# Linear attention and a gated feed-forward layer in one kernel: more of the matrix products in seven sub-products, set 5 turned by TensorE, and another order of the work

## The chip, the cores and the metric

The kernel runs on one core of one Trainium2 chip. The metric is the device time of one execution in microseconds (us); lower is better. Engines are named as in the profile: PE is TensorE's matmul, PEld its weight load, DVE is VectorE, ACT is ScalarE, POOL is GpSimd, SP is SyncE.

## The reference

Cut to what matters:

```python
# q, k, v: (4, 8, 768, 64) float32; lam: (8,); moe_w_in: (512, 2048); moe_w_out: (2048, 512)
for b in range(12):                                   # blocks of 64 tokens
    qb, kb, vb = (q[:, :, sl], k[:, :, sl], v[:, :, sl])
    intra = einsum('bhic,bhjc->bhij', qb, kb) * Dmask  # Dmask = lam ** (i - j) below the diagonal
    intra = einsum('bhij,bhjd->bhid', intra, vb)
    inter = einsum('bhid,bhde->bhie', qb * lam_pow, kv_state)
    out[:, :, sl] = intra + inter
    kv_state = lam_block * kv_state + einsum('bhsd,bhse->bhde', kb * rev_pow, vb)
x = out.transpose(0, 2, 1, 3).reshape(3072, 512)
h = x @ w_in                                          # 512 -> 2048
g = h * (1.0 / (1.0 + exp(-h)))                       # silu
y = g @ w_out                                         # 2048 -> 512, float32, the output
```

## The kernel before

Work is in **units** of 128 tokens, (n, b): pair n of blocks of batch b, six pairs for each of four batches, 24 units. Attention is done in 12 **sets** of two units: sets 0 to 3 hold the units (0, b) and (1, b) of batch b, whose state is carried within the set; sets 4 to 11 hold two batches of one n. The feed-forward layer's first product is done in **groups**: four groups of two units (256 columns), then four of four units (512 columns), one for each n from 2 to 5; what the text calls block 4 is the group with n = 4, and the last block the one with n = 5.

Stages of a set. The loads of q, k and v (`raw`, L380) are issued on SP's queue. `kq` holds k and scaled q in bf16 (casts and multiplications on DVE or ACT), `vd` the scaled v (L349, two halves). `kqT` is kq turned: sets before TURNED = 5 by TensorE transposes (`tr`, L513 for the paired sets, L693 for later ones) and copies from PSUM by DVE and ACT; the others by a DMA transpose on SP's queue (L702). `d_ps` is the state's increment (L534), `y` and `xf` the running states in float32, `xe` the states cast to bf16 (on ACT, DVE or POOL), `st_ps` the scores, which DVE multiplies by the mask into `st` (L349). `x_ps` is the attention's output (L614 and L619 for paired sets, L759 and L767 for the others; L619 and L767 hold the part from the states), copied to `xt`.

First product, L905: `h_ps` over 4 steps of 128 rows of w_in; silu on ACT (L917) makes `g`. The last group (n = 5) is done **in seven**: both operands are split into quadrants, and seven products of quadrants or of sums of quadrants, 128 matmul rows by 256 columns each (L1023), give the four quadrants of the result after some additions. The sums S1 to S4 of w_in's quadrants are tiles `wsum`, the sums T1 to T4 of xt's are `xsum`; part-results are kept as `m` and added to `h`.

Second product: units 0 to 7 (PLAIN = 8) plainly, 16 matmuls of 512 columns a unit (`o_ps`, L940). The other 16 units in seven, four units at a time (L1153): sums of g (`s`, and S3 in place in `g`) by DVE, sums of w_out (`wsum`, halves of 128 x 1024). Results go out through `osb` by DMAs on ACT's queue.

Every step is entered into a planner as a task with a key, its possible engines with their costs, its buffers and what it depends on. The planner simulates the engines and three DMA queues and at each step takes the ready task with the least key whose buffers are free; the result is one list, written out as each engine's order. Engines run in that order at run time. Costs such as those of DMA kinds (SMALL, LARGE, ...), the opening constants (SLOW, FIRST) and the keys therefore set the order, not the time itself. Where PE has nothing ready in the opening, filler matmuls of the identity (L1236) are put in.

The weights are loaded by POOL's queue (L409), each load held behind a small POOL instruction that reads a tile whose landing it awaits (L360); SP's queue is held in the same way by a small DMA. The order of the loads is one string:

```python
SEQUENCE = "s0 i0@0.2 s1 i1a@0.2 i1b i2 i3 o0 o1 s2@1.2 o2 o3 s3 s4"
```

(s is a set's loads, i and o are parts of w_in and w_out.)

Of the kernel before, what the change touches and what calls it, by code (L numbers as in the profile page):

```python
# [216 lines left out]
def kernel(  # L217
# [27 lines left out]
    FRESH, TURNED, ALONE, LEAD = 4, 5, 6, 6.5  # L245
# [3 lines left out]
    BY_POOL, IN_BY_POOL, PLAIN, SPARED = (), (), 8, 1  # L249
# [4 lines left out]
    SCORED, SOON, VD_ON, HALVED = (0, 1), 3, {"DVE": 0.7}, 0  # L254
    EAGER, CALM, ON = 8.0, 1.0, 6.0
# [94 lines left out]


# [16 lines left out]
    def load_set(key, si):  # L368
        n, b = sets[si][0]
        nb = 2  # L370
        rs = [Buf("rb") if si >= CASTING and i == 0 else None if si >= CASTING and i == 1 else Buf("ra" if si in (0, 3) else "rb")
              for i in range(3)]
        ts = []
        x = [t[b, :, 0:2 * U, :].rearrange("h (p e) d -> p h (e d)", e=2) if n < PAIRED else
             t[b:b + 2, :, n * U:n * U + U, :].rearrange("b h s d -> s (b h) d") for t in (k, q, v)]

        def go(e, i):
            if n < PAIRED:
                tile_of(rs[i], [128, H, 2, 64], F32, "raw")
                nc.sync.dma_start(out=rs[i].tile.rearrange("p h e d -> p h (e d)"), in_=x[i])  # L380
            elif si >= CASTING and i < 2:
                tl = tile_of(rs[0], [128, 2, 2, NP, 2, 64], BF16, "kq")
                nc.gpsimd.dma_start(out=tl[:, i].rearrange("p b m h d -> p (b m h) d"), in_=x[i])
            else:
                nc.sync.dma_start(out=tile_of(rs[i], [128, 2 * H, 64], F32, "raw"), in_=x[i])

        for i in (1, 0, 2) if si in QUERIES else range(3):
            if si >= CASTING and i < 2:
                t = pool_task(add((key, i), {"POOL": 0.8}, lambda e, i=i: go(e, i), bufs=[rs[0]], nbytes=0.524, kind=CAST,
                                  prior=pool_last[-1:] + raw[si - 1][1][2], late=2.0))  # L390
                ts.append([t])
                continue
            ts.append([add((key, len(ts)), {"SP": 0.55}, lambda e, i=i: go(e, i), bufs=[rs[i]], nbytes=0.524, prior=sp_last[-1:],
                           kind=WIDE if n < PAIRED else SMALL, late=0.3 if si < FRESH else 3.0)])
# [7 lines left out]
    def load_w(key, what, j, part):  # L402
        def go(e):
# [3 lines left out]
            else:  # L407
# [4 lines left out]
                          HALF if part else LARGE, prior=pool_last[-1:], late=1.0))  # L412
# [7 lines left out]
    for m, x in enumerate(SEQUENCE.split() + [f"s{i}" for i in range(len(sets))]):  # L420
# [59 lines left out]
    def prepare_2(o, rs, lk, lq, lv):  # L480
# [5 lines left out]
        def cast(e, i, a):  # L486
            src = rs[i].tile[:, :, a, :].rearrange("p (m h) d -> p m h d", h=2)
            if i:
# [5 lines left out]
        o.ck = [[add((s - (2.95 if i and o.si in SCALED else 1.0), i), {"DVE": 0.7} if i else {"DVE": 0.45, "ACT": 0.63}, lambda e, i=i, a=a: cast(e, i, a),  # L494
# [3 lines left out]
        def scale_v(e, a):  # L498
            hs = slice(4 * a, 4 * a + 4)
            tt(e, o.vd_of()[:, hs].rearrange("p h e d -> p (h e) d"), rs[2].tile[:, hs].rearrange("p h e d -> p (h e) d"),  # L500
               lam_v2[:, hs].rearrange("p h e -> p (h e)")[:, :, None].to_broadcast([128, 8, 64]), AL.mult)

        o.cv = [add((s - 0.8, 0), VD_ON, lambda e, a=a: scale_v(e, a), deps=lv, bufs=[rs[2], o.vd]) for a in range(2)]
# [19 lines left out]
    def first_2(o):  # L523
# [26 lines left out]
        def blocks(xe, i, src, t, buf):  # L550
# [5 lines left out]
            return [add((s - 0.9, 5), {"POOL": 0.5, "ACT": 0.42}, lambda e, r=r: go(e, r), deps=[t], bufs=[xe, buf])  # L556
# [9 lines left out]
        def rest():  # L566
# [6 lines left out]
            t2 = add((s - 0.9, 5), {"DVE": 0.42}, lambda e: tt(e, xf_of(), y.tile, rate, AL.mult), deps=[t1], bufs=[y, xf_n])  # L573
# [5 lines left out]
        deps = [t for t in o.turned]  # L579
        o.masked = []  # L580
        for g in range(2):
# [9 lines left out]
            ts = add((s - 0.5, g), {"PE": 0.4}, scores, deps=deps, bufs=st_ps[g] + [o.kqT])  # L591
# [42 lines left out]
    def prepare(si):  # L634
# [28 lines left out]
        def cast(e, j, i):  # L663
            src = rs[i].tile[:, j * H:j * H + H, :]
            dst = kq_of()[:, i, j].rearrange("p m h d -> p (m h) d")
            if i:
# [4 lines left out]
        ck = [[add((s - 1.0, i), {"DVE": 0.7} if i else {"DVE": 0.45, "ACT": 0.63}, lambda e, j=j, i=i: cast(e, j, i),  # L671
# [4 lines left out]
        def scale_v(e, j):  # L676
            tt(e, vd_of()[:, j], rs[2].tile[:, j * H:j * H + H, :], lam_v[:, :, None].to_broadcast([128, H, 64]), AL.mult)

        cv = [add((s - 0.8, 0), VD_ON, lambda e, j=j: scale_v(e, j),
# [114 lines left out]
    def after_first(o, t):  # L794
# [20 lines left out]
        def blocks(b, src, deps, bufs, i):  # L815
# [6 lines left out]
            return [add((s - 0.9, i), {"POOL": 0.25 + w / 1000, "ACT": 0.2 + w / 1200, "DVE": 0.1 + w / 1900}, lambda e, r=r: go(e, r),  # L822
# [65 lines left out]
    def product1(gi):  # L888
# [5 lines left out]
        for m0 in range(0, KO, 2 * per):  # L894
# [69 lines left out]
    def sums_of_w_in():  # L964
        bufs = {name: Buf("kq") if i else Buf("rb") for i, name in enumerate(("S1", "S2", "S3", "S4"))}
# [4 lines left out]

        every = [t for o in infos if rank[o.n, o.bs[0]] < SUMS_AFTER for t in o.cv] + [t for o in infos[:CASTING] for ts in o.ck for t in ts]

        def total(name, a, b, op, deps, on):
            done[name] = [add((on, 8), {"POOL": 2.4} if name in IN_BY_POOL else {"DVE": 0.7}, lambda e, ks=ks: tt(
                e, W[name]()[:, ks], W[a]()[:, ks], W[b]()[:, ks], op), deps=deps, bufs=[bufs[name]])
# [9 lines left out]
    def product1_spared(gi, wbufs, wdone):  # L985
# [20 lines left out]
        total("T1", "B12", "B11", AL.subtract, done["T3"], [])  # L1006
        total("T4", "B21", "T2", AL.subtract, done["T2"], [two])
        for jp in range(4):
            P, R = Buf("bank"), Buf("bank")
            held = [P, R, Buf("sp")]  # L1010
# [24 lines left out]
            narrow = {"22": Buf("vd"), "12": Buf("st")}  # L1035
# [175 lines left out]
    for gi in range(len(groups) - SPARED):  # L1211
        product1(gi)
# [60 lines left out]
```

## Time and profile before

| | us |
|---|---|
| median of 3 runs | 204.46 |
| lowest and highest run | 204.32, 205.02 |
| the profiled execution | 204.46 |
| its span | 202.4 |
| PE busy (share of the span) | 188.1 (93%) |
| DVE busy | 135.5 (67%) |
| ACT busy | 114.2 (56%) |
| POOL busy | 21.8 (11%) |

Every profile row is one group or one piece of the kernel's timeline. Rows of the chain of waits read: start in us, length in us, engine, tile, line, and how many instructions. Rows of the groups read: line, engine, operation, tiles out<-in, shape, count, then busy us and the mean ns of one, then the idle time before them with what ended it. Rows of the timeline read: start, length, engine, line, operation, and in brackets the idle time before it. A matmul's busy time in the groups includes its drain, which overlaps the next one; what a matmul costs in a stream is read from the chain.

### The profile page before, as it was taken

How to read it: one execution, taken by the hardware profiler on the slowest of the kernel's cores; microseconds unless marked ns; L12 is line 12 of the kernel's file. 1: busy time of each engine (PE TensorE's matmuls, PEld its weight loads, DVE VectorE, ACT ScalarE, POOL GpSimd, SP SyncE). 2: the span in 40 equal slices, each digit the busy share in tenths (PEclk: the TensorE clock that was granted, in tenths of full speed). 3: DMA queues.
4: the chain of work that ended last, by engine and by line, in shares of the span. 5: the costliest groups of instructions: out<-in, count | busy, mean ns of one | idle time of the engine just before them, and what ended most of it. 6: DMA issues, size and time to landing. Idle time of an engine off the chain costs nothing.

```text
span 202.4 us, 5779 instructions
## 1 busy us (share of the span) xinstructions
PE 188.1 (93%) x2494; PEld 135.0 (67%) x2512; DVE 135.5 (67%) x269; ACT 114.2 (56%) x207; POOL 21.8 (11%) x48
## 2 busy tenths in 40 slices
PE   0588999999999999999999999999999999999992
PEld 0476788557678655544488746486676778888881
DVE  6499620595997950969999774999577553646511
ACT  3836666327567642357764394945656575685320
POOL 6093100310110100001011000110200000000000
PEclk9999999999999999999999999999999999999998
DMA  3999999999999989999999999948001111003313
GB/s 94 301 274 202 216 215 250 254 193 212 239 269 242 206 204 261 174 267 212 202 142 231 253 194 222 225 104 160 2 3 55 52 52 36 19 0 107 104 50 108
DMA packets 87067, 33.40 MB, mean 165 GB/s; under 512 B 65026, under 2 KB 86018, under 8 KB 87042
## 3 DMA queue, kind: packets, MB, share of 16 engines
q1 hardware_dynamic: 77154, 23.07, 57.0%
q0 software_dynamic: 4752, 4.19, 12.9%
q10 hardware_dynamic: 5136, 5.77, 8.9%
q8 instruction: 19, 0.31, 0.7%
q14 instruction: 6, 0.05, 0.1%
HBM read 27.27 MB, written 6.29 MB: 166 GB/s over the span
## 4 chain that ended last, share of the span: by engine, by line
PE 84%; DVE 6%; DMA 4%; ACT 3%; issue 1%; DVEq 0%; SPq 0%
PE h_ps L905 33%; PE o_ps L1153 22%; PE o_ps L940 14%; PE h_ps L1023 6%; DMA raw<-in_k_dram 3%; DVE st L349 2%; PE x_ps L767 2%; PE d_ps L727 1%; PE tr L513 1%; PE x_ps L759 1%; DVE vd L349 1%; PE st_ps L737 1%; DMA out_dram<-osb 1%; ACT xt L342 1%; DVE kqT L344 1%
## 5 line engine op out<-in xcount | busy, mean ns | idle before, releaser
L905 PE MATMUL h_ps<-xt,w_in_bf 128*128 128x256 bf16 (+1 forms) x440 | 73.7, 317 | 0.7 <-ACT xt L342 0.3
L905 PEld LDWEIGHTS <-w_in_bf 128*128 128x128 bf16 x448 | 42.9, 98 | 24.9 <-issue 0.3
L917 ACT ACTIVATE g<-h_ps 128x512 bf16<-128x512 f32 x80 | 46.8, 595 | 20.9 <-PE h_ps L905 20.3
L940 PE MATMUL o_ps<-w_out_bf,g 128*128 128x512 bf16 x118 | 28.6, 379 | 0.8 <-issue 0.5
L1153 PEld LDWEIGHTS <-g 128*128 128x128 bf16 x256 | 25.0, 98 | 3.7
L349 DVE TENSOR_TENSOR st<-st_ps,tri 128x512 bf16<-128x512 f32 x32 | 20.3, 682 | 9.3 <-PE st_ps L737 9.3
L1153 PEld LDWEIGHTS <-s 128*128 128x128 bf16 x192 | 18.7, 98 | 2.8
L349 DVE TENSOR_TENSOR kq<-raw,lam_q 128x512 bf16<-128x512 f32 x24 | 16.3, 698 | 6.2 <-DMA raw<-in_q_dram 4.5
L940 PEld LDWEIGHTS <-g 128*128 128x128 bf16 x128 | 12.0, 98 | 12.0
L349 DVE TENSOR_TENSOR osb<-o_ps,m 128x512 f32<-128x512 f32 (+1 forms) x15 | 8.6, 581 | 13.4 <-ACT m L342 8.6
L342 ACT ACTIVATE xt<-x_ps 128x512 bf16<-128x512 f32 x16 | 9.7, 631 | 12.3 <-PE x_ps L767 9.2
L349 DVE TENSOR_TENSOR vd<-raw,lam_v 128x512 bf16<-128x512 f32 x24 | 15.7, 682 | 0.7 <-DMA raw<-in_v_dram 0.7
L1153 PE MATMUL o_ps<-w_out_bf,s 128*128 128x256 bf16 x128 | 15.3, 273 | 0.0
L1153 PE MATMUL o_ps<-wsum,g 128*128 128x256 bf16 x128 | 15.1, 273 | 0.0
L1153 PE MATMUL o_ps<-w_out_bf,g 128*128 128x256 bf16 x128 | 14.8, 273 | 0.0
L342 ACT ACTIVATE osb<-o_ps 128x512 f32<-128x512 f32 (+1 forms) x13 | 7.3, 564 | 12.7 <-PE o_ps L940 8.6
L349 DVE TENSOR_TENSOR s<-g 128x512 bf16<-128x512 bf16 x16 | 7.2, 447 | 10.8 <-ACT g L917 8.1
L342 ACT ACTIVATE m<-o_ps 128x512 f32<-128x512 f32 (+1 forms) x13 | 6.7, 515 | 13.1 <-PE o_ps L1153 12.9
L513 PE MATMUL tr<-ident,kq 128*128 128x128 bf16 x64 | 6.1, 241 | 7.7 <-DVE kq L349 7.5
L342 ACT ACTIVATE kq<-raw 128x512 bf16<-128x512 f32 x14 | 8.4, 624 | 4.5 <-DMA raw<-in_k_dram 4.0
L346 POOL CAST xe<-xf 64x256 bf16<-64x256 f32 (+1 forms) x8 | 5.1, 640 | 49.4 <-DVE xf L349 39.3
L513 PEld LDWEIGHTS <-kq 128*128 128x128 bf16 x64 | 4.6, 107 | 8.4 <-DVE kq L349 7.9
(90 smaller groups left out, 225.0 us busy)
## 6 DMA issues: line engine op xcount, KB each, us to landing
raw<-in_q_dram SPq DMA_DIRECT2D x12, 512.0 KB, 8.2
raw<-in_k_dram SPq DMA_DIRECT2D x12, 512.0 KB, 7.9
raw<-in_v_dram SPq DMA_DIRECT2D x12, 512.0 KB, 7.2
out_dram<-osb ACTq DMA_DIRECT2D x20, 256.0 KB, 4.2
w_out_bf<-in_moe_w_out_dram POOLq DMA_DIRECT2D x4, 512.0 KB, 14.9
w_in_bf<-in_moe_w_in_dram POOLq DMA_DIRECT2D x3, 512.0 KB, 11.7
w_in_bf<-in_moe_w_in_dram POOLq DMA_DIRECT2D x2, 256.0 KB, 8.2
out_dram<-osb ACTq DMA_DIRECT2D x4, 128.0 KB, 1.7
```

Source lines behind the costliest of these rows:

```text
L342: nc.scalar.activation(o, i, AF.Copy)
L344: nc.vector.tensor_copy(o, i)
L346: nc.gpsimd.tensor_copy(o, i)
L349: (nc.vector if e == "DVE" else nc.gpsimd).tensor_tensor(o, a, b, op=op)
L513: nc.tensor.transpose(t[:, m, a], o.kq_of()[:, i, m, a], ident)
L727: nc.tensor.matmul(d_of(c)[rp, j, m, :], lhsT=o.kq_of()[r, 0, j, m, p, :], rhs=o.vd_of()[r, j, 2 * m + p, :], start=j == 0 and m == 0, sto ...
L767: nc.tensor.matmul(x_of(c)[:, j, m, :], lhsT=o.xe[c].tile[:, (bs[0] + j) % 2, m, :], rhs=o.kqT_of()[:, 1, j, m, halves[c]], start=False, s ...
L905: nc.tensor.matmul(t[:, j, :], lhsT=w_in_bf[:, ko, 128 * (m1 + j):128 * (m1 + j) + 128], rhs=xt[gi].tile[:, ko, :], start=(ko == 0), stop= ...
L917: nc.scalar.activation(t[:, half * per:half * per + per], bank.tile, AF.Silu)
L940: nc.tensor.matmul(t, lhsT=g.tile[:, j, 128 * gp:128 * gp + 128], rhs=w_out_bf[:, ko, :], start=(ko == 0), stop=(ko == KO - 1))
L1023: nc.tensor.matmul(t[:, j, :], lhsT=W[w]()[:, k2, f:f + 128], rhs=X(r)[:, k2, :], start=first and j == 0 and k2 == 0, stop=True, skip_grou ...
L1153: nc.tensor.matmul(t[:, i_, :], lhsT=src(j)[:, k2, 128 * r:128 * r + 128], rhs=W[w]()[:, 2 * j + k2, :], start=first and i_ == 0 and j == ...
```

## The change

* Units 4 to 7 go from the plain second product to the one in seven (PLAIN from 8 to 4).
* Half of block 4's first product (the index pairs 0 and 1, MIXED) is done in seven, the rest as before; `product1` takes the list of row tiles, `product1_spared` the list of its parts.
* TURNED goes from 5 to 6: set 5 is turned by TensorE.
* Casts of states to bf16 have no GpSimd among their engines (XE_2, XE_B, XE_P).
* The keys of later sets are moved back by two (LEAD), the sums of w_out forward (ON from 6 to 0), the second step of a state's update back (LAZY).
* Scores depend on the turned halves they read and not on all of them (FINE).
* Costs in the planner change: LARGE, PART, SLOW, FIRST, SAFE, and the small DMA that holds SP's queue.
* Buffers: kept part-results of block 4 lie in other pools than those of the last block; T1 of xt has a tile of its own where it was made in place; three of the four sums of w_in lie in rb.

The diff, cut to its core:

```diff
-SMALL, WIDE, CAST, LARGE, HALF, TURN = (256, 17.5, 20.0), (512, 25.0, 28.0), (256, 14.0, 31.0), (2048, 88.0, 90.0), (1024, 58.0, 58.0), (1024, 50.0, 50.0)
+SMALL, WIDE, CAST, LARGE, HALF, TURN, PART = (256, 17.5, 20.0), (512, 25.0, 28.0), (256, 14.0, 31.0), (2048, 86.0, 86.0), (1024, 58.0, 58.0), (1024, 50.0, 50.0), (1024, 45.0, 45.0)
...
-    SLOW, SLOWER = 15.5, 1.8
+    SLOW, SLOWER = 14.0, 1.8
...
-    FIRST, LAST, AHEAD = {"SP": 1.9, "ACT": 1.15, "POOL": 2.5}, 1.0, 0.75
+    FIRST, LAST, AHEAD = {"SP": 1.7, "ACT": 1.15, "POOL": 3.0}, 1.0, 0.75
...
-    FRESH, TURNED, ALONE, LEAD = 4, 5, 6, 6.5
+    FRESH, TURNED, ALONE, LEAD = 4, 6, 6, 4.5
...
-    BY_POOL, IN_BY_POOL, PLAIN, SPARED = (), (), 8, 1
+    BY_POOL, PLAIN = (), 4
...
-    SCORED, SOON, VD_ON, HALVED = (0, 1), 3, {"DVE": 0.7}, 0
-    EAGER, CALM, ON = 8.0, 1.0, 6.0
+    SCORED, SOON, HALVED = (0, 1), 3, 0
+    ON_ACT = ()
+    LAZY, FINE, SAFE = 2.0, True, 0.3
+    XE_2, XE_B, XE_P = {"ACT": 0.42, "DVE": 0.35}, 0.1, False
+    MIXED, APART, KEPT = (0, 1), 1, "yf"
+    EAGER, CALM, ON = 8.0, 1.0, 0.0
...
-                held = [add((m - 100, -1), {"SP": 0.15}, lambda e, g=gates, tile=tile: nc.sync.dma_start(
+                held = [add((m - 100, -1), {"SP": 2.2}, lambda e, g=gates, tile=tile: nc.sync.dma_start(
...
-            return [add((s - 0.9, 5), {"POOL": 0.5, "ACT": 0.42}, lambda e, r=r: go(e, r), deps=[t], bufs=[xe, buf])
+            return [add((s - 0.9, 5), XE_2, lambda e, r=r: go(e, r), deps=[t], bufs=[xe, buf])
...
-            t2 = add((s - 0.9, 5), {"DVE": 0.42}, lambda e: tt(e, xf_of(), y.tile, rate, AL.mult), deps=[t1], bufs=[y, xf_n])
+            t2 = add((s + LAZY, 5), {"DVE": 0.42}, lambda e: tt(e, xf_of(), y.tile, rate, AL.mult), deps=[t1], bufs=[y, xf_n])
...
-            ts = add((s - 0.5, g), {"PE": 0.4}, scores, deps=deps, bufs=st_ps[g] + [o.kqT])
+            ts = add((s - 0.5, g), {"PE": 0.4}, scores, deps=o.turned[g::2] if FINE else o.turned, bufs=st_ps[g] + [o.kqT])
...
-            return [add((s - 0.9, i), {"POOL": 0.25 + w / 1000, "ACT": 0.2 + w / 1200, "DVE": 0.1 + w / 1900}, lambda e, r=r: go(e, r),
+            return [add((s - 0.9, i), dict({"ACT": 0.2 + w / 1200, "DVE": XE_B + w / 1900}, **({"POOL": 0.25 + w / 1000} if XE_P else {})), lambda e, r=r: go(e, r),
...
-    def product1(gi):
+    def product1(gi, tiles=None):
...
-        for m0 in range(0, KO, 2 * per):
+        for m0 in tiles or range(0, KO, 2 * per):
...
-        bufs = {name: Buf("kq") if i else Buf("rb") for i, name in enumerate(("S1", "S2", "S3", "S4"))}
+        bufs = {name: Buf("kq" if name == "S3" else "rb") for name in ("S1", "S2", "S3", "S4")}
...
-    def product1_spared(gi, wbufs, wdone):
+    def product1_spared(gi, wbufs, wdone, parts):
...
-        for jp in range(4):
+        closing = gi == len(groups) - 1
+        for jp in parts:
...
-            narrow = {"22": Buf("vd"), "12": Buf("st")}
+            narrow = {"22": Buf("vd" if closing else "y"), "12": Buf("st" if closing else "y")}
...
-            b2, c2 = keep("kqT", [m6])
+            b2, c2 = keep("kqT" if closing else "kq", [m6])
...
-            b3, c3 = keep("xf", [m7])
+            b3, c3 = keep("xf" if closing else KEPT, [m7])
...
-    for gi in range(len(groups) - SPARED):
+    for gi in range(len(groups) - 2):
...
+    left = [j for j in range(4) if j not in MIXED]
+    if left:
+        product1(len(groups) - 2, [m for j in left for m in (2 * j, 2 * j + 8)])
+    if MIXED:
+        product1_spared(len(groups) - 2, *made, MIXED)
+    product1_spared(len(groups) - 1, *made, range(4))
```

Lines of the changed kernel that answer to those above: L905 is L933, L940 is L968, L1023 is L1051, L1153 is L1181, L349 is L353, L342 is L346, L513 is L535, L693 is L721, L702 is L730.

More of the change, by code (lines that the diff above doesn't have):

```diff
@@ L492, in cast @@
                 copy(e, o.kq_of()[:, i, :, a], src)
-        o.ck = [[add((s - (2.95 if i and o.si in SCALED else 1.0), i), {"DVE": 0.7} if i else {"DVE": 0.45, "ACT": 0.63}, lambda e, i=i, a=a: cast(e, i, a),
+        o.ck = [[add((s - (2.95 if i and o.si in SCALED else 1.0), i), by_act("q", o.si, a) if i else {"DVE": 0.45, "ACT": 0.63}, lambda e, i=i, a=a: cast(e, i, a),
                      deps=(lk, lq)[i], bufs=[rs[i], o.kq]) for a in range(2)] for i in range(2)]
@@ L578, in first_2 @@
             rest()
-        deps = [t for t in o.turned]
         o.masked = []
@@ L665, in cast @@
             dst = kq_of()[:, i, j].rearrange("p m h d -> p (m h) d")
-            if i:
+            if i and e != "DVE":
+                for h in range(H):
+                    by_rate(e, dst[:, h], src[:, h], lam_q[:, h:h + 1])
+            elif i:
                 tt(e, dst, src, lam_q[:, :, None].to_broadcast([128, H, 64]), AL.mult)
@@ L669, in cast @@
                 copy(e, dst, src)
-        ck = [[add((s - 1.0, i), {"DVE": 0.7} if i else {"DVE": 0.45, "ACT": 0.63}, lambda e, j=j, i=i: cast(e, j, i),
+        ck = [[add((s - 1.0, i), by_act("q", si, j) if i else {"DVE": 0.45, "ACT": 0.63}, lambda e, j=j, i=i: cast(e, j, i),
                    deps=(lk, lq)[i], bufs=[rs[i], o.kq]) for i in range(2)] for j in range(nb)]
```

54 lines of the change are left out of this document (35 added, 19 removed).

## The prediction

> **What bounds the kernel now.** I read the engines' shares first, then the strip of busy tenths, the chain of waits, and the windows by stage.
>
> ```profile
> PE 188.1 (93%) x2494; PEld 135.0 (67%) x2512; DVE 135.5 (67%) x269; ACT 114.2 (56%) x207; POOL 21.8 (11%) x48
> ...
> PE   0588999999999999999999999999999999999992
> ...
> PE 84%; DVE 6%; DMA 4%; ACT 3%; issue 1%; DVEq 0%; SPq 0%
> ```
>
> TensorE is busy for 93% of the span and carries 84% of the chain. The strip shows two stretches without it at full: the opening (the first four to five slices of 5 us) and the last slice. The chain tells where the full stretch starts and ends.
>
> ```profile
> 19.52 2.40 DVE st L349 x4
> 21.91 0.34 DVE y L349
> ...
> 23.68 0.64 ACT xt L342
> 24.32 0.04 issue
> 24.36 6.28 PE h_ps L905 x56
> ...
> 186.43 8.75 PE o_ps L1153 x80
> ...
> 196.49 1.89 DMA out_dram<-osb
> ```
>
> From 24.36 us the chain lies on PE up to about 195.2; in front of it stands VectorE's and ScalarE's work on set 0. Is PE really gapless in between? The windows (stretch, its length, then the busy time of PE, PEld, DVE, ACT, POOL) say so:
>
> ```profile
> 24.00:56.00 32.00, 31.32 (x387) 22.64 (x391) 17.42 (x34) 18.16 (x33) 3.46 (x6) 1.00 1.09 226
> 56.00:103.00 47.00, 46.47 (x670) 27.55 (x676) 35.14 (x67) 27.43 (x47) 2.35 (x3) 1.00 1.07 222
> 103.00:157.00 54.00, 53.74 (x782) 37.11 (x785) 43.50 (x84) 32.59 (x59) 5.27 (x6) 1.00 0.79 146
> 157.00:196.00 39.00, 38.95 (x344) 33.57 (x344) 20.17 (x44) 22.07 (x41) 0.00 (x0) 1.00 0.14 48
> sum 172.00, PE 170.47 PEld 120.88 DVE 116.23 ACT 100.25 POOL 11.07; mean PE 42.62 PEld 30.22 DVE 29.06 ACT 25.06 POOL 2.77
> ```
>
> PE idles 172.00 - 170.47 = 1.53 us of 172, at a granted clock of 1.00. So work taken from PE here shortens the time one for one, work added lengthens it, and nothing else can gain more than 1.53 us. VectorE has room everywhere (43.50 of 54.00 in its fullest stage). The profiled execution took 204.46 us, its span is 202.4, 2.06 lie around it; the median of the runs is 204.46 too, so the sum is made against both at once.
>
> **The change part by part.** First the prices of a matmul, from the chain:
>
> ```profile
> 71.48 1.73 PE o_ps L940 x8
> 113.26 1.75 PE o_ps L1153 x16
> 150.63 1.73 PE h_ps L905 x8
> 172.90 1.75 PE h_ps L1023 x16
> 59.33 0.45 PE tr L693 x8
> ```
>
> A matmul of 512 columns costs 1.73/8 = 0.2163 us, one of 256 columns 1.75/16 = 0.1094, in both products, and eight transposes 0.45.
>
> *Units 4 to 7's second product in seven.* Four units cost 4 x 16 = 64 matmuls of 512 columns; in seven they cost 112 of 256. -64 x 0.2163 + 112 x 0.1094 = -13.84 + 12.25 = -1.59 us.
>
> *Half of block 4's first product in seven.* 32 matmuls of 512 columns go, 56 of 256 come: -6.92 + 6.13 = -0.79 us.
>
> *Set 5 turned by TensorE.* Sixteen transposes come: 2 x 0.45 = +0.90 us. Its DMA transpose (one of seven on SP's queue) goes. Eight more filler matmuls lie in PE's idle time before 24 us and cost nothing; were that cover gone, they would cost less than the eight transposes' 0.45.
>
> PE's sum: -1.59 - 0.79 + 0.90 = **-1.48 us**.
>
> *Elementwise work.* The sums of g for four more units are 16 operations on VectorE, four more sums are of xt, and the kept products of block 4 add copies and adds:
>
> ```profile
> L349 DVE TENSOR_TENSOR s<-g 128x512 bf16<-128x512 bf16 x16 | 7.2, 447 | 10.8 <-ACT g L917 8.1 <-ACT g L1047 2.5
> ...
> L349 DVE TENSOR_TENSOR h<-h_ps,m 128x512 f32<-128x512 f32 x8 | 5.5, 687 | 4.5 <-ACT m L342 4.5
> ...
> L344 DVE CAST xe<-yf 64x512 bf16<-64x512 f32 x6 | 2.5, 421 | 0.2
> ...
> L342 ACT ACTIVATE m<-h_ps 128x512 f32<-128x512 f32 x8 | 4.8, 595 | 4.4 <-PE h_ps L1023 4.4
> ```
>
> 20 x 0.447 + 4 x 0.687 + 13 more casts of states on VectorE at about 0.42 = 17.2 us spread over the 172; in 56 to 103, where the new sums of g and the casts mostly fall, I count some 8 us on top of 35.14, 43 of 47. VectorE stays below full, so this costs nothing on average; what it costs in waits is below. The end of GpSimd's casts takes a cost away from VectorE, as two rows show:
>
> ```profile
> 104.94 0.65 POOL L346 CAST xe<-yf 64x512 bf16<-64x512 f32 x1 [8.90 <-PE o_ps L1153]
> 105.03 0.83 DVE L349 TENSOR_TENSOR g<-g 128x512 bf16<-128x512 bf16 x1
> ```
>
> While GpSimd casts, a sum of g takes 0.83 us in place of the 0.447 mean. The change has no such cast left.
>
> *The opening.* The chain before 24.36 runs kqT, xt, vd, four masks, y, xf, cast, xt. In the changed order set 0's second xt goes from VectorE to ScalarE:
>
> ```profile
> 17.26 0.64 DVE xt L344
> ```
>
> That takes 0.64 from VectorE ahead of the masks, but the turned copy of q which ScalarE does there comes later behind it, the first state's cast (0.25 to 0.42) is now VectorE's between y and xf (no row has that shape there; half the elements of the 0.421 above or as much), and the masks wait for PE's scores. I have the masks 0.24 earlier and the cast eating half of that: dense PE at 24.25, **-0.1 us**; ends: -0.3 (all of the masks' lead) and +0.3 (the cast whole, no lead). The weights' and the first sets' loads stand on SP and POOL in the same order behind the same gates, so the landings stay. Two other moves change the DMA picture only later: set 5's transpose leaves SP's queue, and the rest were early already:
>
> ```profile
> L702 SPq DMA_TRANSPOSE kqT<-kq x7: 1657/4957/6349, 69.5 to 137.4; - x7
> ...
> DMA to landing us min/median/max: 4.7/6.5/10.0
> ```
>
> For set 6, laying the changed order out with this trace's durations, I estimate the queue's issue at about 77 and the need at 87.5, above the slowest 10.0 us: nothing waits.
>
> *New waits at set 3.* The sums of w_out now stand much earlier in VectorE's order: two of their halves between set 3's two vd, four more before its masks. Rows:
>
> ```profile
> 35.73 1.58 SPq L380 DMA_DIRECT2D raw<-in_v_dram  x1
> raw<-in_v_dram SPq DMA_DIRECT2D x1, 512.0 KB, 13.7
> 36.39 1.50 POOL L409 DMA_DIRECT2D w_out_bf<-in_moe_w_out_dram  x2
> DMA to landing us min/median/max: 8.8/10.5/12.1
> 48.86 0.68 DVE L349 TENSOR_TENSOR wsum<-w_out_bf 128x1024 bf16<-128x1024 bf16 x1
> 49.46 1.29 DVE L349 TENSOR_TENSOR vd<-raw,lam_v 128x512 bf16<-128x512 f32 x2
> 51.19 0.37 PE d_ps L534 x32
> 56.69 0.57 PE x_ps L614 x32
> ```
>
> v lands at 35.73 + 13.7 = 49.43 and the first vd starts at 49.46; the second, behind two halves, ends at 49.46 + 4 x 0.6 = 51.9 (a half takes 0.68 alone, some 0.6 in a row, as the next one began 0.60 behind it). PE asked for it at 51.19 and now has eight matmuls of 512 columns (0.87) more in front: 51.19 + 0.87 - 0.1 = 52.0. No wait, by 0.1. Behind it the four halves (2.4), two masks (1.2), y (0.34) and two masks end at 57.0 (51.9 + 2.4 + 1.2 + 0.34 + 1.2); PE wants the last pair for the latter half of x_ps, at 56.69 + 0.28, less the 0.15 that PE is ahead by then, 56.83: **+0.2 us**. Queued behind these on VectorE are q's casts of set 4, whom nobody awaits for microseconds.
>
> *New wait at set 5.* PE's transposes bring two copies and, in the changed order, xt of set 5 by two copies of ScalarE (1.08 for two):
>
> ```profile
> 147.82 1.08 ACT L342 ACTIVATE xt<-x_ps 128x512 bf16<-128x512 f32 x2 [2.36 <-PE x_ps L767]
> ```
>
> Under them lie eight matmuls (0.87) where sixteen lay before: **+0.1 us**, ends 0 and 0.2.
>
> The hand-overs inside block 4's seven (bank to keep copy to next product) have 0.04 to 0.6 us to spare each at ScalarE's 0.595 a copy (m<-h_ps above). Taken at 0, with their end in a rival. All waits together: +0.3, ends 0 and 1.2. The tail from 186.43 on is the same structure: nothing.
>
> **Sum**: -1.48 - 0.1 + 0.3 = -1.28; 204.46 - 1.28 = **203.2 us**, a span of 201.1. By the ends of opening and waits alone: -1.48 - 0.3 + 0 = 202.7 and -1.48 + 0.3 + 0.3 = 203.6 for the likeliest case (waits at their middle).
>
> **The rivals.** *More gain.* Of the 1.53 us that PE idles, part is a wait on casts of states and on sums slowed as at 105.03; without GpSimd these go. Half of the 1.53 back and no new wait: 204.46 - 1.48 - 0.1 - 0.75 = 202.1. Against it: the sums themselves grow in number. 0.10.
>
> *Hand-overs.* Block 4's half in seven makes PE wait for each kept copy as ScalarE has silu, copies of xt and casts in the same queue. Of 14 hand-overs, if each lacks 0.06 us, 0.8: 204.0. For it: the margins of 0.04; against: in the last block the same pattern ran gapless (38.95 of 39.00). 0.16, of which 0.06 stays over 0.3% faster.
>
> *Slower: a load in front of VectorE.* The second half of the w_out sums needs the last part of w_out, and set 3's second vd is queued behind it, with PE's d_ps waiting for that. w_out's last part is issued at 37.14 (the second of the two from 36.39) and landed at most 12.1 us later, 49.2; its sum starts at 50.7. Slack 1.4 us; slower by 0.3% begins 1.87 us above the forecast, thus at a landing 15.4 us after issue. The first pair of the same loads shows that it can be:
>
> ```profile
> w_out_bf<-in_moe_w_out_dram POOLq DMA_DIRECT2D x1, 512.0 KB, 17.6
> ```
>
> At 17.6: 54.7 + 0.6 (sum) + 0.6 (vd) = 55.9 in place of 52.0: +3.9, 207.1. Against it: the same transfers in the same order are ahead of it. 0.12.
>
> *Narrow matmuls cost more than half.*
>
> ```profile
> L1153 PEld LDWEIGHTS <-g 128*128 128x128 bf16 x256 | 25.0, 98 | 3.7
> ```
>
> If a quarter of a weight load (98 ns) were uncovered at each added matmul of 256 columns, 168 x (0.1094 + 0.0245) = 22.5 against 96 x 0.2163 = 20.8 removed, with 0.9 for transposes and the 0.2: 207.3. The 16 in 1.75 were measured with their loads, so 0.02. The page "TensorE: Matmul & The Clock Gate" of the Trainium skill, section "Back-to-back issue gap", states a rule that speaks against this change: in a sustained stream 81 ns a matmul at 128 columns and 131 ns at 512, so that wide ones come far below their share. Interpolated (an estimate from that page) 256 columns would cost 98 ns: 168 x 0.098 - 96 x 0.131 = +3.9, near 209 with the transposes. The trace disagrees: 216 and 109 ns in one and the same stream.
>
> That the change does not do what it says has no chance: the counts of instructions in its built order are those used above.
>
> **How the numbers follow.** Forecast 0.60 (203.2; its own range 202.7 to 203.6), more gain 0.10, hand-overs 0.16, late load 0.12, narrow matmuls 0.02. A difference of 0.3%, 0.61 us, is about what a measurement here can tell from none: faster is below 203.85, slower above 205.07. Faster 0.60 + 0.10 + 0.06 = 0.76; same 0.10; slower 0.14. The range leaves out the slow cases and takes in the gain's 202.1 and the hand-overs (204.0); with the bad ends of opening and waits together, -1.48 + 0.3 + 1.2, it ends at 204.5: 202.1 to 204.5.
>
> **What would show it.** Right: the windows from 24 to about 195 with PE's busy share unchanged and its sum about 1.5 us lower; 112 more matmuls of 256 columns at line 1181 and 56 more at 1051, at 1.75 us for 16; sixteen transposes in 0.9; dense PE from 24.2 to 24.4; no idle time of PE over 0.3 us at set 3's d_ps and x_ps or at set 5's xt; sums of g without 0.8 us cases. Wrong: a wait on DVE vd or st near 52 to 57 (late load), repeated short waits on m or g around block 4's first product (hand-overs), 16 matmuls in clearly over 1.75 (narrow), or a dense start that has moved by more than 0.3 us, which I hold the least certain of the small terms.

## The result, and the profile after

The changed kernel takes 202.94 us (median of 6 runs, 202.53 to 203.59); the kernel before, run beside it, 204.74 (204.32 to 205.16). The ratio is 0.9917, with a 95% interval of 0.9895 to 0.9938: 0.8% faster, 1.8 us by the medians and 1.3 to 2.1 by the interval. The forecast was 203.2. The profiled execution took 203.13 us, its span is 201.4 (201.43 to two places, where the kernel before had 202.37).

The page of the kernel after, the lines that answer to those of before:

```profile
PE 188.2 (93%) x2608; PEld 143.3 (71%) x2608; DVE 147.2 (73%) x304; ACT 119.6 (59%) x224; POOL 11.5 (6%) x33
...
PE   0488999999999999999999999999999999999993
...
PE 76%; DVE 15%; DMA 4%; ACT 2%; issue 1%; SPq 0%; DVEq 0%
```

TensorE has as large a share of the span as before. VectorE's busy time grew by 11.7 us and GpSimd's shrank by 10.3. The chain now runs over VectorE for 15% of the span, not 6%. Where does it leave PE? The chain of waits of the kernel after:

```profile
24.09 0.74 DVE xt L348
...
24.87 7.16 PE h_ps L933 x64
...
88.50 1.27 DVE st L353 x2
...
107.66 0.69 DVE osb L353
...
108.40 3.65 PE o_ps L1181 x32
...
186.03 12.24 PE o_ps L1181 x112
```

From 88.5 to 108.4 us the chain runs over VectorE's work alone. That does not mean that PE stood still there, as the windows of the kernel after show (same columns as before):

```profile
24.00:56.00 32.00, 31.81 (x392) 22.41 (x390) 17.95 (x34) 19.55 (x37) 1.87 (x3) 1.00 1.14 237
56.00:103.00 47.00, 46.93 (x748) 33.85 (x746) 42.93 (x88) 31.29 (x58) 0.00 (x0) 1.00 1.09 222
103.00:157.00 54.00, 53.87 (x777) 40.15 (x775) 45.76 (x92) 30.19 (x56) 0.00 (x0) 1.00 0.68 139
157.00:196.00 39.00, 39.00 (x382) 33.28 (x381) 22.17 (x51) 24.41 (x46) 0.00 (x0) 1.00 0.11 37
sum 172.00, PE 171.61 PEld 129.69 DVE 128.82 ACT 105.44 POOL 1.87; mean PE 42.90 PEld 32.42 DVE 32.20 ACT 26.36 POOL 0.47
```

From 56 to 103 us VectorE is at 42.93 of 47.00 where it was at 35.14, while PE is at 46.93. PE's busy share is no measure of its waits, though: the ends of its matmuls are modelled, and a short wait hides in a stretched row. So I account for the profiled execution in another way. PE's dense start is the matmul from which it runs on without a long gap. Its work after that is counted from the built order, with prices read from the chain as in the prediction; what the dense stretch is longer than this is its waits (all stretches that nothing accounts for included). All in us, from each run's own profile:

| run | dense start, behind the first cast of k | dense stretch of PE | counted work in it | waits | last matmul to end of span |
|---|---|---|---|---|---|
| before | 24.36, 16.39 | 174.30 | 173.69 | 0.61 | 3.71 |
| after | 24.87, 16.32 | 173.39 | 172.20 | 1.19 | 3.17 |

The work fell by 1.49 and the waits rose by 0.58. The first load of k landed 0.58 later in this one profile (its cast starts at 8.55 where it started at 7.97); in the profiles of seven variants of the changed kernel the cast started at 7.99 to 8.17, so that lateness is not the change's. The end of the span came 0.54 sooner behind the last matmul. Sum: 0.58 - 0.07 - 0.91 - 0.54 = -0.94, the difference of the spans.

Not all of the 1.8 us lies in the span. Of the kernel before, 2.01 to 2.14 us of each run that was timed beside the experiments lie outside it; of the kernel after, 1.66 to 1.73 in its six runs. That is some 0.36 us which no count of work or waits holds.

### The profile page after: what moved, and what is told of

Same layout as the page of the kernel before. It is cut to its first block, busy times and chain, and to the rows that moved or that the text cites. A ratio compares the mean times of both kernels' runs of the same rounds, so it can differ in the third digit from the quotient of the medians.

```text
span 201.4 us, 6016 instructions
## 1 busy us (share of the span) xinstructions
PE 188.2 (93%) x2608; PEld 143.3 (71%) x2608; DVE 147.2 (73%) x304; ACT 119.6 (59%) x224; POOL 11.5 (6%) x33
## 4 chain that ended last, share of the span: by engine, by line
PE 76%; DVE 15%; DMA 4%; ACT 2%; issue 1%; SPq 0%; DVEq 0%
PE h_ps L933 25%; PE o_ps L1181 25%; PE h_ps L1051 9%; PE o_ps L968 7%; DVE st L353 4%; DMA raw<-in_k_dram 4%; DVE s L353 2%; PE x_ps L795 2%; DVE vd L353 2%; PE tr L535 1%; DVE xe L348 1%; PE d_ps L755 1%; DVE y L353 1%; DVE osb L353 1%; PE x_ps L787 1%
## 5 line engine op out<-in xcount | busy, mean ns | idle before, releaser
L933 PE MATMUL h_ps<-xt,w_in_bf 128*128 128x256 bf16 (+1 forms) x416 | 66.6, 314 | 0.3 <-DVE xt L348 0.2
L933 PEld LDWEIGHTS <-w_in_bf 128*128 128x128 bf16 x416 | 39.9, 98 | 21.1 <-DVE xt L348 0.5
L945 ACT ACTIVATE g<-h_ps 128x512 bf16<-128x512 f32 x72 | 41.6, 593 | 21.2 <-PE h_ps L933 20.7
L1181 PEld LDWEIGHTS <-g 128*128 128x128 bf16 x320 | 31.2, 98 | 4.5
L1181 PEld LDWEIGHTS <-s 128*128 128x128 bf16 x240 | 23.4, 98 | 3.4 <-issue 0.3
L353 DVE TENSOR_TENSOR st<-st_ps,tri 128x512 bf16<-128x512 f32 x32 | 20.4, 680 | 3.1 <-PE st_ps L765 3.1
L353 DVE TENSOR_TENSOR osb<-o_ps,m 128x512 f32<-128x512 f32 (+1 forms) x18 | 10.7, 599 | 14.4 <-ACT m L346 8.8
L346 ACT ACTIVATE m<-o_ps 128x512 f32<-128x512 f32 (+1 forms) x17 | 9.1, 533 | 20.2 <-PE o_ps L1181 16.8
L353 DVE TENSOR_TENSOR kq<-raw,lam_q 128x512 bf16<-128x512 f32 x24 | 16.0, 682 | 6.3 <-DMA raw<-in_q_dram 4.0
L1181 PE MATMUL o_ps<-w_out_bf,s 128*128 128x256 bf16 x160 | 19.1, 273 | 0.1
L1181 PE MATMUL o_ps<-wsum,g 128*128 128x256 bf16 x160 | 18.9, 273 | 0.0
L1181 PE MATMUL o_ps<-w_out_bf,g 128*128 128x256 bf16 x160 | 18.6, 273 | 0.0
L353 DVE TENSOR_TENSOR vd<-raw,lam_v 128x512 bf16<-128x512 f32 x24 | 15.8, 681 | 1.8 <-DMA raw<-in_v_dram 1.8
L968 PE MATMUL o_ps<-w_out_bf,g 128*128 128x512 bf16 x64 | 15.8, 379 | 0.0
L346 ACT ACTIVATE xt<-x_ps 128x512 bf16<-128x512 f32 x17 | 10.5, 646 | 8.0 <-PE x_ps L795 7.2
L353 DVE TENSOR_TENSOR h<-h_ps,m 128x512 f32<-128x512 f32 x12 | 8.3, 688 | 7.6 <-ACT m L346 6.4
L535 PE MATMUL tr<-ident,kq 128*128 128x128 bf16 x64 | 6.1, 242 | 8.0 <-DVE kq L353 7.9
L346 ACT ACTIVATE kq<-raw 128x512 bf16<-128x512 f32 x19 | 11.5, 624 | 3.4 <-DMA raw<-in_k_dram 3.3
L535 PEld LDWEIGHTS <-kq 128*128 128x128 bf16 x64 | 4.5, 108 | 9.1 <-DVE kq L353 8.2
L1051 PEld LDWEIGHTS <-wsum 128*128 128x128 bf16 x96 | 9.4, 98 | 1.3
L353 DVE TENSOR_TENSOR s<-g 128x512 bf16<-128x512 bf16 x20 | 8.2, 417 | 2.8 <-ACT g L1075 1.1
L348 DVE COPY kqT<-tr 128x512 bf16<-128x512 bf16 x11 | 4.6, 422 | 7.3 <-PE tr L535 4.2
```

The source lines that it names most:

```text
L346: nc.scalar.activation(o, i, AF.Copy)
L348: nc.vector.tensor_copy(o, i)
L353: (nc.vector if e == "DVE" else nc.gpsimd).tensor_tensor(o, a, b, op=op)
L535: nc.tensor.transpose(t[:, m, a], o.kq_of()[:, i, m, a], ident)
L933: nc.tensor.matmul(t[:, j, :], lhsT=w_in_bf[:, ko, 128 * (m1 + j):128 * (m1 + j) + 128], rhs=xt[gi].tile[:, ko, :], start=(ko == 0), stop= ...
L945: nc.scalar.activation(t[:, half * per:half * per + per], bank.tile, AF.Silu)
```

## The experiments

Every kernel was timed in five rounds beside the kernel before on the same chip. A planner lays out the order, so an edit moves other work too; only the first run has the changed kernel's order untouched.

**Is PE's work the time? (e1)** Set 5's transposes twice:

```diff
+                    for _ in range(2 if si == 5 else 1):
                         for i in range(2):
                             for m in range(NP):
                                 nc.tensor.transpose(t[:, i, m, :], kq_of()[:, i, j, m], ident)
```

> The changed kernel with set 5's sixteen transposes on TensorE issued twice (the second pass writes the same values); every engine's order is otherwise untouched. Theory A, that TensorE's work sets the time one for one: the added 16 x 0.056 = 0.90 us come out whole, 202.9 + 0.9 = 203.8 us, and the dense end of PE moves by 0.9. Rival B, that the gain came from waits and the opening and PE has slack at set 5: 0 to 0.3, at most 203.2.

Measured 203.31 us, ratio 0.9955 (0.9935 to 0.9976), against 0.9917 for the changed kernel: +0.0038, 0.8 us of the 0.9. In the profile counted work rose by 0.89 and waits fell from 1.19 to 0.92, so that the dense stretch grew by 0.62. The two ratio intervals just overlap; together with the profile, theory A holds for most of it.

**Block 4's first product: none, half or all in seven (e2, e3).**

```diff
-    MIXED, APART, KEPT = (0, 1), 1, "yf"
+    MIXED, APART, KEPT = (), 1, "yf"              # e2
+    MIXED, APART, KEPT = (0, 1, 2, 3), 1, "yf"    # e3
```

> The changed kernel with block 4's first product wholly plain again (MIXED empty): 32 matmuls of 512 columns in place of 56 of 256, +0.79 us of PE's work by the chain's prices. The plan is the same up to PE's first matmul in seven of that block. Theory A: 202.9 + 0.8 = 203.7. Rival C, that the hand-overs of block 4's seven give the 0.79 back as waits: 202.9 or less.

> The changed kernel with all of block 4's first product in seven (MIXED 0 to 3): another 32 matmuls of 512 columns become 56 of 256, -0.79 us of PE's work. Theory A: 202.9 - 0.8 = 202.1. Rival C (hand-overs, or VectorE's and ScalarE's added copies and adds, wait in front of PE): 202.9 or more.

Without it: 203.48, ratio 0.9950 (0.9935 to 0.9965), +0.0033 or 0.7 us; counted work +0.80, waits 1.17 for 1.19. The intervals just overlap here too, and the profile sides with theory A: the work came back and no waits went. With all of it: 203.20, ratio 0.9940 (0.9921 to 0.9958): no gain. Work fell by another 0.80 and waits rose to 2.33. The timeline of this run shows them on PE (in brackets the idle time and what ended it) and, below, VectorE's queue in the same microseconds:

```profile
152.49 0.60 PE L1051 MATMUL h_ps<-xt,w_in_bf 128*128 128x256 bf16 x4
153.34 0.60 PE L1051 MATMUL h_ps<-xsum,w_in_bf 128*128 128x256 bf16 x4 [0.25 <-ACT m L346]
153.83 0.60 PE L1051 MATMUL h_ps<-xt,w_in_bf 128*128 128x256 bf16 x4
154.60 0.60 PE L1051 MATMUL h_ps<-xt,wsum 128*128 128x256 bf16 x4 [0.18 <-DVE h L353]
...
151.20 0.69 DVE L348 COPY m<-h_ps 128x512 f32<-128x512 f32 x1
151.86 0.43 DVE L353 TENSOR_TENSOR s<-g 128x512 bf16<-128x512 bf16 x1
152.25 0.69 DVE L348 CAST xt<-x_ps 128x512 bf16<-128x512 f32 x1
152.86 0.41 DVE L353 TENSOR_TENSOR s<-s,g 128x512 bf16<-128x512 bf16 x1
153.19 0.42 DVE L353 TENSOR_TENSOR g<-g 128x512 bf16<-128x512 bf16 x1
153.53 0.42 DVE L353 TENSOR_TENSOR s<-g,s 128x512 bf16<-128x512 bf16 x1
153.86 0.68 DVE L353 TENSOR_TENSOR h<-h_ps,m 128x512 f32<-128x512 f32 x1
```

Four matmuls of 256 columns take 0.44; from 152.49 to 153.34 and from 153.83 to 154.60 PE gives 0.85 and 0.77 for four. At 153.34 it had waited for a kept copy on ScalarE (m). At 154.60 it had waited for the add h, which stands on VectorE behind four sums of g and a cast of xt. These two account for 0.74 of the 1.14 us. That is the prediction's rival of the hand-overs, in the second half of the block: it is real, and the half that the change takes stays clear of it.

**Set 5 by DMA again (e4), and units 4 to 7 in seven alone (e5).**

```diff
-    FRESH, TURNED, ALONE, LEAD = 4, 6, 6, 4.5
+    FRESH, TURNED, ALONE, LEAD = 4, 5, 6, 4.5             # e4, in the kernel after
-    BY_POOL, IN_BY_POOL, PLAIN, SPARED = (), (), 8, 1
+    BY_POOL, IN_BY_POOL, PLAIN, SPARED = (), (), 4, 1     # e5, in the kernel before
```

> The changed kernel with set 5 turned by a DMA transpose again (TURNED 5): sixteen transposes leave PE, -0.90 us. Theory A: 202.0 us, if the turned tile lands before the scores of set 5 ask for it. Rival D: the DMA transpose (median 6.5 us from issue to landing in the kernel before) lands late or its place moves the sets behind it, PE waits, and the time stays at 202.9 or rises; then TensorE's turning pays its 0.90 in waits avoided.

> The kernel before with one part of the change: units 4 to 7's second product in seven (PLAIN 4), casts of states still on GpSimd, sets as early as before, set 5 by DMA transpose. Theory A (TensorE's work): -1.59 us, 204.4 - 1.6 = 202.8. Rival E (this part pays only with the others: VectorE's 16 sums of g more, beside GpSimd's casts, stand in front of what PE waits for, as in the run with set 5 by DMA): PE waits, 203.6 to 207.

e4: 206.63, ratio 1.0104 (1.0089 to 1.0119), 3.8 us slower than the changed kernel with 0.89 us less work on PE; waits 4.80. e5: 205.26, ratio 1.0053 (1.0033 to 1.0073), 0.8 slower than before by the medians and 1.1 by the ratio with 1.59 less work; waits 3.34. Both wait longest in the first product in seven of units 4 to 7, in e4 from 74.6:

```profile
74.63 0.60 PE L1181 MATMUL o_ps<-w_out_bf,s 128*128 128x256 bf16 x4
76.49 1.60 PE L1181 MATMUL o_ps<-w_out_bf,s 128*128 128x256 bf16 x12 [1.26 <-DVE s L353]
...
74.14 1.28 DVE L353 TENSOR_TENSOR kq<-raw,lam_q 128x512 bf16<-128x512 f32 x2
75.34 0.42 DVE L353 TENSOR_TENSOR g<-g 128x512 bf16<-128x512 bf16 x1
75.68 0.42 DVE L353 TENSOR_TENSOR s<-g,s 128x512 bf16<-128x512 bf16 x1
76.02 0.75 DVE L353 TENSOR_TENSOR s<-g 128x512 bf16<-128x512 bf16 x2
```

Not the turned tile is late but the sums: two multiplications of q for a later set stand in VectorE's queue ahead of them. Rival D's outcome, by another mechanism than the landing that it named. This wait is 1.26 of e4's 4.80 us; the next ones behind it are on ScalarE's copies m (0.68 and 0.46, at 81.32 and 84.63) and on an add h (0.78, at 153.96). And 1.28 us of e4's loss are no waits at all: its span ends 4.45 us behind the last matmul and not 3.17, which is taken up under the tail below.

**GpSimd's casts (e6, e7, e12).**

```diff
-... {"POOL": 0.5, "ACT": 0.42}
+... {"ACT": 0.42, "DVE": 0.35}                        # e6, sets 0 to 3; later sets without POOL too
+... {"DVE": 0.35} if r else {"ACT": 0.42}             # e12 in place of it
-    XE_2, XE_B, XE_P = {"ACT": 0.42, "DVE": 0.35}, 0.1, False
+    XE_2, XE_B, XE_P = {"POOL": 0.5, "ACT": 0.42}, 0.1, True   # e7, in the kernel after
```

> The kernel before with no cast of states on GpSimd (the fifteen casts go to VectorE and ScalarE, at 0.42 and 0.6), nothing else changed. Theory A: PE's work is unchanged, so 204.4 within 0.3. Rival B (GpSimd's casts slowed VectorE and made PE wait, and their end is a gain of its own): up to 0.8 us faster, 203.6.

> The changed kernel with GpSimd among the engines for casts of states again (15 casts there). PE's work is unchanged. Theory A: 202.9 within 0.3. Rival B: VectorE's sums run at 0.83 in place of 0.42 us while a cast runs, VectorE is near full between 56 and 103 us (42.93 of 47.00), so PE waits: 203.5 or more.

> The kernel before with no casts of states on GpSimd, but in sets 0 to 3 one cast of each pair on VectorE and the other on ScalarE. The run without GpSimd lost 1.1 us, all ahead of PE's dense start, where ScalarE did both casts of a pair one behind the other (0.41 each, twice) and GpSimd had done one beside it. Theory H (that is the whole loss): the dense start comes back to 16.4 us behind the landing of the first k, and the time to 204.4 within 0.4. Rival I (VectorE is the next in line, as it is the chain there): 0.3 us for each cast on the chain, 204.9 or more.

e6: 205.46, ratio 1.0045 (1.0033 to 1.0057), 0.9 us slower: neither theory. Its dense start stands 17.50 behind the first cast of k, not 16.39, and the chain says why:

```profile
23.93 0.42 ACT xe L342
...
24.36 0.41 ACT xe L342
...
24.80 0.75 ACT xt L342
...
25.59 0.49 PE h_ps L905 x3
```

ScalarE does both casts of a pair in a row where GpSimd did one beside it. e12, with a cast of each pair on VectorE, comes back to 204.66, ratio 1.0011 (0.9995 to 1.0027), dense 16.67 behind: theory H, but for 0.28 us at the start. e7: 202.99, ratio 0.9940 (0.9916 to 0.9963); its interval holds the changed kernel's 0.9917, so with the other parts of the change in place the casts on GpSimd make no difference that these runs can tell. Its one profile has 0.59 us more waits (1.78), whose source stays open. Rival B's condition did come up in it (one cast took 3.96 us), but nobody waited for that.

**The sums of w_out late (e8).**

```diff
-    EAGER, CALM, ON = 8.0, 1.0, 0.0
+    EAGER, CALM, ON = 8.0, 1.0, 6.0
```

> The changed kernel with the sums of w_out at the later key of before (ON 6): they are made between and behind set 3's masks and not ahead of them. PE's work, the POOL queue and the SP queue are the same. Prediction's step at set 3: the early sums cost 0.2 us there, so 202.7 to 202.9. Rival: the sums come too near to the first product in seven, or push the sums of g back in VectorE's fullest stage: 203.2 or more.

202.48 us, ratio 0.9904 (0.9891 to 0.9917), waits 0.92. That is 0.3 us below the changed kernel by the ratios and 0.5 by the medians, which is not the rival's outcome, but the intervals overlap. If there is a gain, it is not at set 3, where the prediction's step had it: from PE's dense start to the d_ps of set 4, with the same work in between, PE took 37.34 us in the kernel after (24.87 to 62.21) and 37.33 in e8 (24.49 to 61.82). It is the fastest version here by median: clearly faster than before, not clearly faster than the change.

**Units 4 to 7 in seven with set 5 turned by TensorE, in the kernel before (e9, e10).**

```diff
-    BY_POOL, IN_BY_POOL, PLAIN, SPARED = (), (), 8, 1
+    BY_POOL, IN_BY_POOL, PLAIN, SPARED = (), (), 4, 1
-    FRESH, TURNED, ALONE, LEAD = 4, 5, 6, 6.5
+    FRESH, TURNED, ALONE, LEAD = 4, 6, 6, 6.5    # e9; LEAD 4.5 in e10
```

> The kernel before with units 4 to 7's second product in seven and set 5 turned by TensorE. PE's work: -1.59 + 0.90 = -0.69 us. Theory F (the wait of 1.7 us on the sums of g near 75 us, and those behind it, came because a set that is turned by DMA needs its k and q early, so that VectorE did them ahead of the sums): the waits go, 204.4 - 0.7 = 203.7. Rival G (VectorE has simply too much to do there with the sets begun as early as before): waits remain, 205 or more.

> As the run before it, and the later sets begun two units later (LEAD 4.5 in place of 6.5). PE's work is the same, -0.69 us. Theory F: 203.7 already without it, so no difference. Rival G: only this one comes to 203.7.

208.43, ratio 1.0184 (1.0162 to 1.0205), and 208.86, ratio 1.0202 (1.0176 to 1.0228); waits 5.90 and 5.94. Theory F is half right: the wait on the sums near 75 us is gone. A larger one has come, on set 5's output. ScalarE's timeline, PE's and GpSimd's of e9:

```profile
77.37 0.63 ACT L342 ACTIVATE xe<-yf 64x512 bf16<-64x512 f32 x1 [0.35 <-DVE yf L349]
77.91 0.57 ACT L342 ACTIVATE xt<-x_ps 128x512 bf16<-128x512 f32 x1
79.84 0.63 ACT L342 ACTIVATE xe<-xf 64x512 bf16<-64x512 f32 x1 [1.35 <-DVE xf L349]
80.37 0.57 ACT L342 ACTIVATE xt<-x_ps 128x512 bf16<-128x512 f32 x1
...
78.47 0.41 PE L767 MATMUL x_ps<-kqT,xe 128*128 128x64 bf16 x8 [0.89 <-POOL xe L346]
81.00 1.61 PE L905 MATMUL h_ps<-xt,w_in_bf 128*128 128x512 bf16 x4 [2.12 <-ACT xt L342]
...
77.50 0.92 POOL L346 CAST xe<-yf 64x512 bf16<-64x512 f32 x1 [9.31 <-DVE yf L349]
79.90 7.95 POOL L346 CAST xe<-xf 64x512 bf16<-64x512 f32 x1 [1.49 <-DVE xf L349]
```

The second copy of xt stands in ScalarE's queue behind a cast that waits for VectorE's xf, and PE waits 2.12 us for it. Ahead of that, PE waits 0.89 us for a cast of a state on GpSimd. LEAD made no difference, so rival G's reading of e10 falls too. In the kernel after this copy follows the first at once, from 76.96 on and ahead of that cast, and PE has eight matmuls to put over both.

**Three parts of block 4 with the sums late (e11).** MIXED (0, 1, 2) and ON 6.0.

> The changed kernel with the sums of w_out late (as in the run that gave 202.48) and three of the four parts of block 4's first product in seven. PE's work: -0.39 us, 202.1 by theory A. In the run with all four parts PE waited 1.2 us between 150 and 155 us for VectorE's adds and sums; if the third part already meets that wait, 202.5 to 203.2.

202.65, ratio 0.9900 (0.9881 to 0.9920); counted work 0.40 less than in e8, waits 1.70 for 0.92. The third part's gain is gone again in waits.

The account of all runs, in us (time is the median, the rest from the profile):

| run | time | counted work | waits | dense start behind first cast of k | last matmul to end |
|---|---|---|---|---|---|
| e1, transposes twice | 203.31 | 173.09 | 0.92 | 16.32 | 3.14 |
| e2, block 4 plain | 203.48 | 173.00 | 1.17 | 16.33 | 3.17 |
| e3, all of block 4 | 203.20 | 171.40 | 2.33 | 16.34 | 3.15 |
| e4, set 5 by DMA | 206.63 | 171.31 | 4.80 | 16.32 | 4.45 |
| e5, before, units 4 to 7 | 205.26 | 172.10 | 3.34 | 16.39 | 3.62 |
| e6, before, no GpSimd | 205.46 | 173.69 | 0.79 | 17.50 | 3.58 |
| e7, after, with GpSimd | 202.99 | 172.20 | 1.78 | 16.26 | 3.16 |
| e8, sums late | 202.48 | 172.20 | 0.92 | 16.33 | 3.16 |
| e9, e5 and set 5 | 208.43 | 173.00 | 5.90 | 16.39 | 3.16 |
| e10, e9 later | 208.86 | 173.00 | 5.94 | 16.37 | 3.16 |
| e11, three parts | 202.65 | 171.80 | 1.70 | 16.33 | 3.16 |
| e12, before, split | 204.66 | 173.69 | 0.77 | 16.67 | 3.57 |

## Why the prediction was right, point by point

*The whole.* Direction, cost of the work and time came as forecast, 1.8 us gained where 1.28 stood in the sum; but the nearness is in part luck. The terms that the sum had (work, opening, waits) brought -1.49 - 0.07 + 0.58 = -0.98. The rest came from two places that it held unchanged: the end of the span behind the last matmul (-0.54, of which 0.13 is one late store in the profile of before) and the time outside the span (-0.36). So the prediction's reading that nothing but PE's work could gain more than 1.53 us left out what lies behind PE's last matmul.

*Prices and PE's sum, -1.48.* Right. Rows of the kernel after, from its chain:

```profile
67.46 0.45 PE tr L721 x8
...
73.59 1.75 PE o_ps L1181 x16
...
179.05 1.75 PE h_ps L1051 x16
```

The prices are unchanged, and e1 and e2 give 0.8 of 0.90 and 0.7 of 0.79, within their intervals. The counts came too: 560 matmuls at line 1181 where 448 stood, 168 at line 1051 where 112 stood. PE's sum from 24 to 196 us was to fall by 1.5 and rose from 170.47 to 171.61: a fixed window cannot show less work on an engine that goes on with the next. Units 4 to 7's part was not taken back by itself in the kernel after, so its -1.59 stays untried there; in the kernel before (e5) PE's counted work fell by that much while the time rose, so that term of the sum is only what the work costs, not what the edit brings alone.

*The opening, -0.1.* Measured -0.07, from 16.39 to 16.32 behind the first cast. The least certain of the small terms came out, though both of its parts were larger than forecast: against the first cast the masks end 0.40 earlier (forecast 0.24), and from there to the dense start it takes 0.33 longer (forecast 0.12). That they cancel as well as forecast is luck. The dense start itself, at 24.87, lies outside the 24.2 to 24.4 named beforehand, by the late load.

*Set 3, +0.2.* It came out as nothing. v was issued at 36.44 in the kernel after and landed 12.3 us later, at 48.74 and not at 49.4, and what VectorE does from then on is done earlier than forecast:

```profile
48.82 0.69 DVE L353 TENSOR_TENSOR vd<-raw,lam_v 128x512 bf16<-128x512 f32 x1 [1.76 <-DMA raw<-in_v_dram]
49.42 1.29 DVE L353 TENSOR_TENSOR wsum<-w_out_bf 128x1024 bf16<-128x1024 bf16 x2
50.63 0.68 DVE L353 TENSOR_TENSOR vd<-raw,lam_v 128x512 bf16<-128x512 f32 x1
...
55.18 1.29 DVE L353 TENSOR_TENSOR st<-st_ps,tri 128x512 bf16<-128x512 f32 x2
```

The last mask ends at 56.47, in front of PE's x_ps at 56.93: no wait. The order was as predicted; the landing, 0.7 sooner, gave the margin. The late load (0.12) did not occur.

*Set 5's xt, +0.1 (0 to 0.2).* It came, a little above the upper end. Chain and weight loads of the kernel after:

```profile
76.96 1.09 ACT xt L346 x2
...
78.10 6.20 PE h_ps L933 x28
...
78.10 0.53 PEld L933 LDWEIGHTS <-w_in_bf 128*128 128x128 bf16 x3 [0.24 <-issue]
```

The eight matmuls that start at 76.99 give out at 77.86; the two copies end at 78.05 and PE goes on at 78.10: 0.24. PE's own row shows less idle there, by the modelled ends; the weight load's bracket shows it whole.

*All waits, +0.3.* Here the size was off: +0.58, and mostly elsewhere. Compared at each set's d_ps, PE falls behind its counted work by 0.2 us less than before up to 62 us; between 72 and 112 us it loses 0.7 where it lost 0.15. In that stretch VectorE carries the chain; the largest single waits there are 0.24 at set 5's xt and 0.30 at 108.40, behind VectorE's osb. I had costed VectorE's load as free on average. Its size was right where I gave one (43 of 47 from 56 to 103 us, measured 42.93), and yet waits came. That fullness as such makes them is not shown: e8, with 43.81 there, has 0.92 us of waits, and e4 and e9, with 39.94 and 37.62, have 4.80 and 5.90.

*The tail, 0.* It was 0.54 shorter, by a term that I did not have, and the traces show what it is. At the end SyncE goes through a file of nine semaphore waits, among them that for the last store, which goes out on SyncE's own queue; from one wait that is already fulfilled to the next it takes 0.06 us. In us behind the end of the last matmul:

| run | last store issued | wait for that store: place in the file, end | ninth wait ends | span ends |
|---|---|---|---|---|
| before | 0.62 | second, 2.43 | 2.85 | 3.71 |
| after | 0.49 | ninth, 2.31 | 2.31 | 3.17 |

In the kernel before, seven more waits follow when the last store has landed; in the kernel after they were passed while it was under way. That is 0.42 us; the other 0.13 is that the last store was issued later in this one profile of the kernel before. All fourteen profiles divide in the same way. In the five with set 5 turned by DMA (before, e4, e5, e6, e12; 82 transfers) the last store tells its landing by semaphore 100, second in the file, and the span ends 1.27 to 1.29 us behind that wait. In the nine with set 5 turned by TensorE (81 transfers) it is semaphore 118, ninth in the file, and the span ends 0.85 to 0.86 behind it. So a DMA transpose less, in the middle of the kernel, moved the last store to another semaphore and gained 0.42 us at its end; e4 against the kernel after and e9 against e5 differ in this one setting and show it both ways. In e4 the last store was also issued late, 1.36 behind the last matmul.

*Outside the span, 0.* The prediction carried its 2.06 us over unchanged; it is 0.36 shorter. It is 1.66 to 1.78 in every run with units 4 to 7 in seven, also in the kernel before (e5, e9, e10), and 1.78 to 2.14 in the three kernels without (before, e6, e12). What it consists of no trace here shows; it stays open.

*GpSimd.* The row pair of 0.65 and 0.83 us was read as a cost of its own that ends. e6 and e7 show no gain from ending it that their times can tell; in e9 a GpSimd cast did make PE wait, 0.89 us.

## What to carry to other kernels

On a kernel whose matrix engine is full, counted work times the price in the stream predicts the direction; what an edit brings is that less the waits that its elementwise work makes. These are found by laying the new order against what the engine is owed next, queue by queue. The busy share of the second-busiest engine does not tell where: from 56 to 103 us VectorE was busier in the kernel after (42.93 of 47.00, 1.19 us of waits in all) than in e5 (40.87, 3.34) or e9 (37.62, 5.90). Here the same 1.59 us of work less stood in a change that gained, and turned into a loss of 0.8 us alone (e5) and of 4 with one companion (e9), so a part of a planned order cannot be judged outside it. Read waits as dense stretch less counted work: PE's idle time by its rows, from 24 to 196 us, fell from 1.53 to 0.39 while its waits by the count rose from 0.61 to 1.19. And account for the whole time: here some 0.8 of the 1.8 us came from SyncE's last waits and from outside the span.

## What the runs showed of the hardware

GpSimd's cast of 64 x 512 took 0.61 us in e9 at 67.58, where VectorE was idle or read PSUM, and 7.95 us from 79.90 to 87.85, over the whole of a file of VectorE's operations that ended at 87.38; 7.62 in e10. VectorE's own rows in that stretch kept their 0.42 us. The Trainium skill, page "SBUF — State Buffer", section "Who interferes with whom", says that a VectorE instruction with two inputs in SBUF contends with a GpSimd one that reads SBUF, and that the order of issue decides who blocks. The trace agrees, as the cast came second there, and adds that it did not come in between two such instructions: it lasted as long as the file did.

The clock of PE fell after its wait in e9. One window a microsecond of that run (PE's busy time, granted clock, DMA share, GB/s):

```profile
79.00:80.00 1.00, 0.00 (x0) 1.00 0.99 192
80.00:81.00 1.00, 0.00 (x1) 1.00 0.60 123
81.00:82.00 1.00, 0.95 (x4) 0.87 1.15 215
82.00:83.00 1.00, 1.00 (x4) 0.50 1.10 188
83.00:84.00 1.00, 1.00 (x4) 0.50 0.77 135
84.00:85.00 1.00, 1.00 (x4) 0.50 1.20 237
85.00:86.00 1.00, 1.00 (x6) 0.93 0.99 173
```

By these clocks PE lost 0.13 + 3 x 0.50 + 0.07 = 1.7 us, which is the 1.67 by which it fell further behind its counted work there: a wait of 2.1 us was paid nearly twice. At half the clock that is a stretch of 3.4 us, which began some 0.7 us after PE had gone on at 81.00. The Trainium skill, page "TensorE: Matmul & The Clock Gate", section "What's actually happening", gives at least one idle window of about 3.4 us before the clock falls. The trace differs: 2.12 us with a gap of 0.89 ahead of it were enough. Only e9 and e10, the two profiles with this pair of waits, show a granted clock below 1.00 between 24 and 196 us; the waits in e5, of up to 1.7 us, show none.
